# Recurrent attention and a two-level mixture of experts on one core: another order for the routing of two chunks, the first expert weights and the first unit

## The chip, the cores and the metric

One core of one Trainium2 chip runs the whole program. The metric is the device time of one execution in microseconds, as the median of several runs; lower is better. All other times are from one profiled execution of the kernel, counted from the start of its span.

## The reference, cut to what matters

A gated linear recurrence (four sequences, eight heads, 768 steps, head size 48) is followed by a mixture of 16 experts in four groups, in which each of the 3072 tokens goes to one expert.

```python
f = 1.0 / (1.0 + np.exp(-f_logit))
for t in range(S):
    state = f[:, :, t, :, None] * state + np.einsum('bhd,bhe->bhde', k[:, :, t], v[:, :, t])
    y[:, :, t] = np.einsum('bhd,bhde->bhe', q[:, :, t], state)
x = y.transpose(0, 2, 1, 3).reshape(B * S, H * D)          # 3072 x 384
g_idx = argmax(x @ w_group); g_w = softmax at g_idx
e_idx = argmax(x @ w_expert[g_idx]); e_w = softmax at e_idx
out[token] = g_w * e_w * (relu(x @ w1[g, e]) @ w2[g, e])   # 384 -> 1024 -> 384
```

## The kernel before, in words

**Attention.** The 768 steps are cut into six chunks of 128, and a chunk into two units of two sequences each; so there are twelve units, numbered 0 to 11. The work of a unit is written as small Python generators, each of which records a few instructions and yields: `bounded` (`c`, clamps the gate logits, L555), `gated` (`g`: exponential and logarithm on ScalarE, L565 and L568, then the running sum over time as a matmul, `cs`, L574, and two exponentials of it, `eq` and `kh`), `multiplied` (`m`: q times `eq`, L589, and k times `kh`, L592, on VectorE), `turned` (`t`: transposes `tr_q` and `tr_k` on TensorE, L604, copied to SBUF, L605), `decayed` (`b`: transposes `gt` of the row `ends`, L614), `scored` (`s`: the products `ap`, L630, masked into `am` by VectorE, L633), `weighed` (`w`: `y`, first from the state, L669, then from `am` and v, L674, copied to `xT`, L677), `stated` (`n`: the new state, `ds`, L647), `done` (`d`: routing logits `lT`, L689, `lgT`, L691, `lg`, L694) and `listed` (`x`: `x_ps`, L709, copied and written to `x_dram`, L712).

**Order.** The engines TensorE, VectorE and ScalarE run their instructions in the order in which these generators are advanced. That order is written out by hand: the strings `BEGIN`, `EVEN`, `ODD` and `ORDERS` name a generator and an offset to the unit, and `step` advances it once. `r` advances the oldest routing that is under way, `e` the early experts.

**Routing.** When both units of a chunk have their logits, `routed` starts `route` for it. It yields ten times at most: (1) maxima; (2) the one-hot `ohe`, L200; (3) ranks `rk` on TensorE, L205 and L208; (4) slots, `pick` to `run`, L214 to L217; (5) the lane mask `ln`, L227; (6) `head` and `val`, L231 and L234; (7) the weights and `meta`, L237 to L247, written to `x_dram`; (8) the table `tb` on TensorE, L252; (9) a ranking of the experts, L272 to L281, in some chunks only; (10) the sum into the table, L257, and what follows it. Chunk 3 (`CLOSE`) is the one after which the two fullest experts are fixed: `choose_early` writes their names into `who` (L290) and their first 128 rows into `rows_e`. With these, SyncE loads the weights of the two experts (`load_weights`, 1536 KB each of first layer `w1` and second layer `w2`, L384 and L386), GpSimd gathers the rows (L394), and `early` computes both experts: `up` (L440, `hp`) for the first and the second, and then `down_rows` (L457, `yo`) for each. Chunk 4's step 4 also runs `fix_early` (L300 to L306), and the last chunk's step 10 `choose`, whose gathers (`rows_p`) begin the sixteen main passes. The passes then take the rest of the time.

**Transfers.** SyncE issues all loads, ScalarE the writes of `x_dram<-x` and of `ends<-eq`, the last row of a unit's decay, which `gt` later transposes. Each of these transfers signals one of eight completion semaphores, which the compiler gives out; before a transfer is issued on a semaphore, its queue waits until the one before it on that semaphore has landed.

Of the kernel before, what the change touches and what calls it, by code (L numbers as in the profile page):

```python
# [10 lines left out]
FP32 = mybir.dt.float32  # L11
# [4 lines left out]
OP = mybir.AluOpType  # L16
AX = mybir.AxisListType.X
ET = mybir.EngineType
P = 128
# [4 lines left out]
def kernel(  # L24
# [12 lines left out]
    nc = tc.nc  # L37
    B, H, S, D = q.shape
    N, DM = out.shape
    G = moe_w_group.shape[1]  # L40
    EG = moe_w_expert.shape[2]
    F = moe_w1.shape[3]
    GE = G * EG
    NC = S // P
    NT = N // P
    HP = H // 2
    DP = 64
    KO = DM // P
    FO = F // P
    NL = G + GE  # L50
    WIDE = 2 * P
    EARLY = 2
# [9 lines left out]
    SAFE = 32.0  # L62
# [6 lines left out]
    wp = ctx.enter_context(tc.tile_pool(name="wp", bufs=2))  # L69
# [4 lines left out]
    w1v = moe_w1.rearrange("g e (ko p) f -> (g e) p ko f", p=P)  # L74
    w2v = moe_w2.rearrange("g e (fo p) d -> (g e) p fo d", p=P)

    def const(shape, dtype, name):
        return cp.tile(shape, dtype, tag=name, name=name)

    def bank(shape, name):  # L80
        return ps.tile(shape, FP32, tag="bank", name=name)
# [9 lines left out]
    ident = const([P, P], FP32, "ident")  # L91
# [170 lines left out]
    who = const([1, GE], I32, "who")  # L262
# [3 lines left out]
    def ranked(np_, sb):  # L266

        def tmp(shape, name):
            return sb.tile(shape, FP32, tag=name, bufs=1, name=name)

        key = tmp([P, GE], "rkey")
        nc.vector.tensor_tensor(key, run, base, OP.subtract)  # L272
        nc.vector.scalar_tensor_tensor(out=key, in0=key, scalar=float(GE), in1=tie, op0=OP.mult, op1=OP.add)
        if np_ > EARLY:
            nc.vector.tensor_tensor(key, key, boost, OP.add)
        less = tmp([P, GE, GE], "less")
        nc.vector.tensor_tensor(less, key.unsqueeze(1).broadcast_to((P, GE, GE)), key.unsqueeze(2).broadcast_to((P, GE, GE)), OP.is_gt)
        rank = tmp([P, GE], "rank")
        nc.vector.reduce_sum(out=rank, in_=less, axis=AX)
        sel = order[:, 0:np_, :]  # L280
        nc.vector.tensor_tensor(sel, rank.unsqueeze(1).broadcast_to((P, np_, GE)), experts[:, 0:np_].unsqueeze(2).broadcast_to((P, np_, GE)), OP.is_equal)  # L281
        return rank
# [30 lines left out]
    def choose_early(sb):  # L313
        number = numbers(sb)
        mine = sb.tile([P, EARLY, GE], FP32, tag="mine2", bufs=1, name="mine2")
        nc.vector.tensor_tensor(mine, order[:, 0:EARLY, :], number[:, :, 0].unsqueeze(1).broadcast_to((P, EARLY, GE)), OP.mult)
        got = sb.tile([P, EARLY], FP32, tag="got2", bufs=1, name="got2")
        nc.vector.reduce_sum(out=got, in_=mine, axis=AX)
        nc.vector.tensor_copy(rows_e, got)
        named(EARLY, sb)  # L320

    def choose(sb):
        number = numbers(sb)
        mine = sb.tile([P, 2, HP, P], FP32, tag="am", bufs=3, name="mine").rearrange("p r a t -> p (r a t)")[:, 0:2 * GE * GE].rearrange("p (n j e) -> p n j e", j=2, e=GE)
        got = sb.tile([P, GE, 2], FP32, tag="got", bufs=1, name="got")
        for j in range(2):
            nc.vector.tensor_tensor(mine[:, :, j, :], order, number[:, :, j].unsqueeze(1).broadcast_to((P, GE, GE)), OP.mult)
        nc.vector.reduce_sum(out=got, in_=mine, axis=AX)
        nc.vector.tensor_copy(rows_p, got)
        named(GE, sb)  # L330
# [47 lines left out]
    def value(ap, top):  # L378
        return nc.values_load(ap, engines=(ET.SP,), min_val=0, max_val=top, skip_runtime_bounds_check_because="a table that the routing makes within these bounds")

    def load_weights(pool, ap):
        e = value(ap, GE - 1)
        w1 = pool.tile([P, KO, F], FP32, tag="w1", name="w1")
        nc.sync.dma_start(out=w1, in_=w1v[bass.ds(e, 1)].rearrange("o p k f -> (o p) k f"))  # L384
        w2 = pool.tile([P, FO, DM], FP32, tag="w2", name="w2")
        nc.sync.dma_start(out=w2, in_=w2v[bass.ds(e, 1)].rearrange("o p k f -> (o p) k f"))  # L386
        return w1, w2

    def fetch(pool, rows, n, top=N):

# [96 lines left out]
    def early():  # L487

        ws = [fetch(ep, rows_e[:, p:p + 1], P, (CLOSE + 1) * B * P) for p in range(EARLY)]
        yield  # L490
        for w in ws:
            turn_in(w)
            yield
        for p, w in enumerate(ws):
            yield from up(w, weights[p][0])
        for p, w in enumerate(ws):
            yield from down_rows(w, weights[p][1])

    weights = {}

    with ExitStack() as fast:
# [27 lines left out]
        NU = len(units)  # L529
# [3 lines left out]
        def heads(t):  # L533
            return t.rearrange("p b h d -> p (b h) d")
# [23 lines left out]
        def gated(i):  # L558
# [13 lines left out]
            for b in range(2):  # L572
# [8 lines left out]
                    nc.scalar.dma_start(out=ends[c][2 * s:2 * s + 2, :], in_=eq[P - 1:P].rearrange("o b h d -> o b (h d)"))  # L581
                yield

        def multiplied(i):

            w = live[i]
            for b in (slice(0, 1), slice(1, 2)) if i < 2 else (slice(0, 2),):
                qh, kh = heads(w["qh"][:, b])[:, :, 0:D], heads(w["kh"][:, b])[:, :, 0:D]
                nc.vector.tensor_tensor(qh, qh, heads(w["eq"][:, b])[:, :, 0:D], OP.mult)  # L589
                yield  # L590

                nc.vector.scalar_tensor_tensor(out=kh, in0=kh, scalar=math.exp(SAFE), in1=heads(w["k"][:, b]), op0=OP.min, op1=OP.mult)  # L592
                yield

        def turned(i):
            w = live[i]
            w["g"] = decays[:, units[i][0], :, 2 * units[i][1]:2 * units[i][1] + 2].rearrange("p a b -> p b a")
            for nm in ("q", "k"):
                w["T" + nm] = sb.tile([P, 2, HP, P], FP32, tag="T" + nm, name="T" + nm)
            for b in range(2):  # L600
                for nm in ("q", "k"):
                    pt = bank([P, HP, P], "tr_" + nm)
                    for a in range(HP):
                        nc.tensor.transpose(out=pt[:, a, :], in_=w[nm + "h"][:, b, 2 * a:2 * a + 2, :].rearrange("t r d -> t (r d)"), identity=ident)  # L604
                    (nc.vector.tensor_copy if i == 0 and b == 0 and nm == "k" else nc.scalar.copy)(w["T" + nm][:, b], pt)  # L605
                    yield

        def decayed(i):

# [105 lines left out]
        def routed(c):  # L715

            yield from route(c, groups[c], sb, tidy=fix_early if c == CLOSE + 1 else None, ranking=rank_early if c == CLOSE else (lambda pool: ranked(GE, pool)) if c == NC - 1 else None)
            if c == CLOSE:
                choose_early(sb)
                for p in range(EARLY):  # L720
                    weights[p] = load_weights(wp, who[0:1, p:p + 1])
                first.append(early())
                next(first[0])
            elif c == NC - 1:
                choose(sb)

        def advance(gens):
            if gens and next(gens[0], True):
                gens.pop(0)

        first, routes = [], []

# [3 lines left out]
        STAGES = {"c": bounded, "g": gated, "m": multiplied, "t": turned, "s": scored, "n": stated, "w": weighed, "d": done, "x": listed, "b": decayed}  # L736
        BEGIN = """c0 g0 p g0 g0 m0 m0 m0 m0 l2 t0 t0 t0 t0 c1 g1 g1 s0 s0 s0 s0 g1 g1 p w0 w0 n0 m1 m1 m1 m1 l3 h x0 x0 x0
            t1 t1 t1 t1 b1 c2 g2 g2 s1 s1 s1 s1 p d0 g2 g2 n0 n1 w1 w1 m2 m2 l4 n1
            d0 x1 x1 t2 t2 t2 t2 c3 g3 g3 x1 s2 s2 s2 s2 g3 g3 w2 d1 w2 n2 m3 m3 c4 g4 g4""".split()
        BEGUN = 3  # L740
        EVEN = "l+2 d-2 n-1 r r r x-1 x-1 t t t t g+1 g+1 x-1 r s s s s c+2 w d-1 g+2 w g+2 n m+1 m+1".split()
        ODD = "l+2 d-2 b n-1 r r x-1 x-1 t t t t g+1 g+1 x-1 r s s s s c+2 w d-1 g+2 w g+2 n m+1 m+1 r n".split()
        ORDERS = {
            NU - 2: "d-2 r r r x-1 x-1 t t t t g+1 g+1 x-1 r s s s s w d-1 w n m+1 m+1 r r".split(),
            NU - 1: "d-2 b n-1 x-1 x-1 r r t t t t x-1 r s s s s r w d-1 w r r".split(),
            NU: "d-2 r e d-1 x-1 x-1 d-1 x-1 r r r e e r e r r e r r e r e r r e e e e e".split(),
        }
        steps_of = {}
# [1 line left out]
        def step(nm, i):  # L750
            if nm == "r":
                advance(routes)
            elif nm == "e":
                next(first[0], None)
            elif nm == "p":
                next(pad)
            elif nm == "h":
                turn_gates()
            elif 0 <= i < NU:
                if nm == "l":  # L760
                    load(i)
                    return
                if (nm, i) not in steps_of:
                    steps_of[nm, i] = STAGES[nm](i)
                next(steps_of[nm, i], None)
# [7 lines left out]
        for tok in BEGIN:  # L773
            step(tok[0], int(tok[1:] or 0))
# [43 lines left out]
    rest = const([1, 1], I32, "rest")  # L818
    ws = {n: pass_of(n) for n in range(3)}
    ahead = {n: load_weights(wq if n % 3 == 1 else wp, who[0:1, PLACES[n]:PLACES[n] + 1]) for n in range(1, 2)}  # L820
    ahead[0] = weights[0]

# [20 lines left out]
    for n in range(GE - 1):  # L843
        w = ws[n]
# [108 lines left out]
    with tc.If(more > 0), ExitStack() as late:  # L953
# [5 lines left out]
        with tc.For_i(0, last, 1) as i:  # L959
            w1, w2 = load_weights(wp, b_expert[0:1, bass.ds(i, 1)])  # L960
# [13 lines left out]
            w = fetch(ep, row, P)  # L974
# [32 lines left out]
```

## Time and profile before

| | |
|---|---|
| time, median of 3 runs | 436.17 us (435.5 to 436.47) |
| span of the profiled execution | 434.2 us |
| TensorE matmuls busy | 409.4 us, 94% |
| VectorE busy | 268.5 us, 62% |
| ScalarE busy | 154.5 us, 36% |
| GpSimd busy | 71.7 us, 17% |
| moved by DMA | 88.97 MB |

How to read the views: the page gives busy time by engine, then the span in 40 slices with busy tenths of each. The table of waits has on each line the waiting instruction, what ended its wait, the sum in us, how often, and the longest. The timeline has start, length, engine, line, operation, tiles and count, and in brackets the idle time ahead of it with what ended it. Neighbours of one kind are merged into one line.

In time order: attention fills 0 to some 142 us, the two early experts 145 to 169 us, and the sixteen passes the rest, with the last write landing at the end.

### The profile page before, as it was taken

The numbers are of one execution on the slowest core, as the hardware profiler recorded it, in microseconds if no ns is written. First come the engines' busy times: TensorE is split into PE (matmuls) and PEld (weight loads), VectorE is DVE, ScalarE is ACT, GpSimd is POOL, SyncE is SP. The second block draws the span as 40 slices with busy tenths as digits, with TensorE's granted clock in tenths as the row PEclk, the third lists the DMA queues.
The fourth block names the chain that finished last, engine by engine and source line by source line (L and its number), as shares of the span: only waits on it lengthen the run. The fifth ranks groups of instructions, "written<-read, shape, count | busy, mean of one in ns | idle before, by whom it ended". The sixth has DMA issues, their size and how long they took to land. (4 is left out here: it accounts for less than half of the span.)

```text
span 434.2 us, 10159 instructions
## 1 busy us (share of the span) xinstructions
PE 409.4 (94%) x4103; PEld 383.8 (88%) x4103; DVE 268.5 (62%) x781; ACT 154.5 (36%) x338; POOL 71.7 (17%) x109
## 2 busy tenths in 40 slices
PE   4999999999998989999999999999999999999960
PEld 2888999889998877989999999999999999999940
DVE  5675786778687841540799759468559558651500
ACT  5676765576664411211123123123123122222200
POOL 3000000000002037101031232212212211022120
PEclk9999999999999999999999999999999999999995
DMA  9999999999815979965728549468459558652010
GB/s 168 175 208 203 186 196 161 219 217 209 159 39 166 404 242 364 394 217 215 255 74 337 170 189 327 151 238 311 158 233 348 174 191 331 239 163 92 25 32 17
DMA packets 135232, 88.97 MB, mean 205 GB/s; under 512 B 105422, under 2 KB 125972, under 8 KB 135178
## 3 DMA queue, kind: packets, MB, share of 16 engines
q1 hardware_dynamic: 126754, 72.38, 61.2%
q0 software_dynamic: 5056, 11.06, 7.6%
q10 hardware_dynamic: 3368, 4.80, 3.1%
q8 instruction: 34, 0.56, 0.6%
q14 instruction: 20, 0.16, 0.1%
HBM read 78.71 MB, written 9.83 MB: 204 GB/s over the span
## 5 line engine op out<-in xcount | busy, mean ns | idle before, releaser
L440 PE MATMUL hp<-xe,w 128*128 128x128 f32 (+14 forms) x864 | 138.6, 320 | 1.6 <-DMA w<-in_moe_w_dram 1.6
L440 PEld LDWEIGHTS hp<-xe,w 128*128 128x128 f32 x864 | 135.8, 190 | 2.5 <-issue 1.7
L472 PE MATMUL yo<-h,w 128*128 128x230 f32 (+13 forms) x672 | 115.8, 333 | 0.0
L472 PEld LDWEIGHTS yo<-h,w 128*128 128x128 f32 x672 | 113.7, 190 | 0.2
L423 DVE STREAM_TRANSPOSE yr<-yT 32x192 f32<-32x192 f32 (+1 forms) x208 | 70.5, 339 | 64.7 <-ACT yT L473 62.1
L441 ACT ACTIVATE h<-hp 128x256 f32<-128x256 f32 (+14 forms) x72 | 34.4, 478 | 110.7 <-PE hp L440 110.7
L416 DVE STREAM_TRANSPOSE xe<-xg 32x192 f32<-32x192 f32 (+1 forms) x208 | 69.7, 335 | 5.0 <-PE hp L440 2.0
L451 POOL DMA_INDIRECT out_dram<-yt,xg x32 | 34.5, 1080 | 154.7 <-ACT yt L448 82.2
L473 ACT COPY yT<-yo 128x230 f32<-128x230 f32 (+13 forms) x42 | 13.5, 326 | 80.5 <-PE yo L472 80.5
L394 POOL DMA_INDIRECT xg<-x_dram,rows_p x30 | 29.6, 988 | 70.4 <-DMA out_dram<-yt,xg 22.8
L633 DVE TENSOR_TENSOR am<-ap,tri 128x512 f32<-128x512 f32 x48 | 29.8, 683 | 18.0 <-PE ap L630 18.0
L574 PE MATMUL cs<-ld_f,tri 128*128 128x384 f32 x48 | 19.2, 526 | 6.2 <-DVE ld_f L555 5.4
L630 PE MATMUL ap<-Tq,Tk 48*64 48x128 f32 x768 | 23.9, 273 | 0.1
L674 PE MATMUL y<-am,v 128*64 128x128 f32 x384 | 23.1, 273 | 0.0
L674 PEld LDWEIGHTS y<-am,v 128*64 128x64 f32 x384 | 21.3, 137 | 0.5 <-DVE am L633 0.5
L630 PEld LDWEIGHTS ap<-Tq,Tk 48*64 48x64 f32 x768 | 20.8, 133 | 1.0 <-issue 0.2
L457 PE MATMUL yo<-w,h 128*128 128x384 f32 x64 | 21.3, 486 | 0.0
L246 POOL COPY meta<-token 128x4 int32<-128x4 int32 x6 | 1.3, 218 | 109.0 <-DMA x_dram<-meta 109.0
L457 PEld LDWEIGHTS yo<-w,h 128*128 128x128 f32 x64 | 11.9, 190 | 7.4
L574 PEld LDWEIGHTS cs<-ld_f,tri 128*128 128x128 f32 x48 | 8.6, 200 | 10.4 <-POOL meta L246 5.4
L448 ACT ACTIVATE yt<-yr,xg 128x384 f32<-128x384 f32 (+13 forms) x26 | 14.4, 604 | 5.4 <-DVE yr L423 5.4
L677 ACT COPY xT<-y 128x512 f32<-128x512 f32 x24 | 12.9, 588 | 8.2 <-PE y L674 8.2
(168 smaller groups left out, 380.4 us busy)
## 6 DMA issues: line engine op xcount, KB each, us to landing
w<-in_moe_w_dram SPq DMA_DIRECT2D x34, 1536.0 KB, 11.0
qh<-in_q_dram SPq DMA_DIRECT2D x12, 384.0 KB, 8.0
ld_k<-in_k_dram SPq DMA_DIRECT2D x12, 384.0 KB, 7.8
v<-in_v_dram SPq DMA_DIRECT2D x12, 384.0 KB, 7.1
x_dram<-x ACTq DMA_DIRECT2D x12, 384.0 KB
ld_f<-in_f_logit_dram SPq DMA_DIRECT2D x11, 384.0 KB, 6.1
out_dram<-yt,xg POOLq DMA_INDIRECT x32, 3.8
xg<-x_dram,rows_p POOLq DMA_INDIRECT x30, 6.6
```

The lines of the kernel that those rows point to most:

```text
L394: nc.gpsimd.indirect_dma_start(out=w["x"][:, j, :], out_offset=None, in_=x_dram[0:1 + top, :], in_offset=bass.IndirectOffsetOnAxis(ap=rows ...
L416: squares(w, lambda n, k_, rk, g, rg: nc.vector.transpose(out=xT[rg, 0:n, k_], in_=x[rk, 0:n, g]))
L423: squares(w, lambda n, k_, rk, g, rg: nc.vector.transpose(out=y[rk, 0:n, g], in_=yT[rg, 0:n, k_]))
L440: nc.tensor.matmul(hp[:, o, :], lhsT=w1[:, ko, (f + o) * P:(f + o + 1) * P], rhs=w["xT"][:, ko, :], start=(ko == 0), stop=(ko == KO - 1))
L441: nc.scalar.activation(h[:, f:f + 2, :], hp, AF.Relu)
L451: nc.gpsimd.indirect_dma_start(out=out, out_offset=bass.IndirectOffsetOnAxis(ap=w["x"][0:m, j, DM + 1:RW].bitcast(U32), axis=0), in_=y[0:m ...
L457: nc.tensor.matmul(yp, lhsT=w["h"][:, fo, :], rhs=w2[:, fo, :], start=(fo == 0), stop=(fo == FO - 1))
L472: nc.tensor.matmul(yp, lhsT=w2[:, fo, m * P:(m + 1) * P], rhs=w["h"][:, fo, :], start=(fo == 0), stop=(fo == FO - 1))
L574: nc.tensor.matmul(cs.rearrange("t h d -> t (h d)"), lhsT=tri, rhs=nl[:, b], start=True, stop=True)
L630: nc.tensor.matmul(ap[r][half, a, :], lhsT=w["Tk"][rows, b, a, half], rhs=w["Tq"][rows, b, a, :], start=True, stop=True)
L633: nc.vector.tensor_tensor(am[:, r], ap[r], tri.unsqueeze(1).broadcast_to((P, HP, P)), OP.mult)
L674: nc.tensor.matmul(ys[r][DP * b:DP * b + DP, a, :], lhsT=w["v"][:, b, 2 * a + r, :], rhs=w["am"][b][:, r, a, :], start=(c == 0 and a == 0) ...
```

## The change

Four things are changed.

1. **Routing of chunks 3 and 4.** In unit 9's order two `r` move ahead of the score products, so that chunk 3's steps 3 to 6 come one place earlier; in unit 10's order the three `r` at its start are then steps 7, 8 and 9 (the ranking, L272 to L281, comes ahead of the mask `am`). In unit 11's order `q q` advances the second routing in the list, chunk 4's steps 1 and 2, and only then `r` takes chunk 3's step 10, which names the early experts. Then chunk 4's steps 3 and 4 come ahead of unit 11's score products, where step 4 stood behind them. The purpose is to have chunk 4's `ohe` ready when TensorE comes to `rk`.
2. **Early experts' weights.** Both numbers are read first, then the two first layers are loaded, and then the two second layers.
3. **First unit.** q of both sequences is multiplied, transposed and copied ahead of k, so that it need not wait for k; all four copies go to ScalarE, where one was VectorE's.
4. **Unit 2.** The first half of `weighed` (from the state) moves ahead of the running sums of unit 3.

```diff
+    def load_layer(pool, e, layer):
+        w = pool.tile([P, KO, F] if layer == 1 else [P, FO, DM], FP32, tag=f"w{layer}", name=f"w{layer}")
+        nc.sync.dma_start(out=w, in_=(w1v if layer == 1 else w2v)[bass.ds(e, 1)].rearrange("o p k f -> (o p) k f"))
+        return w
...
+        def in_order(i, bs):
+            return [(nm, b) for nm in ("q", "k") for b in bs] if i == 0 else [(nm, b) for b in bs for nm in ("q", "k")]
...
-            for b in range(2):
-                for nm in ("q", "k"):
...
-                    (nc.vector.tensor_copy if i == 0 and b == 0 and nm == "k" else nc.scalar.copy)(w["T" + nm][:, b], pt)
+            for nm, b in in_order(i, range(2)):
...
+                nc.scalar.copy(w["T" + nm][:, b], pt)
...
-                for p in range(EARLY):
-                    weights[p] = load_weights(wp, who[0:1, p:p + 1])
+                es = [value(who[0:1, p:p + 1], GE - 1) for p in range(EARLY)]
+                w1s, w2s = ([load_layer(wp, e, layer) for e in es] for layer in (1, 2))
+                weights.update(enumerate(zip(w1s, w2s)))
...
-        def advance(gens):
-            if gens and next(gens[0], True):
-                gens.pop(0)
+        def advance(gens, n=0):
+            if len(gens) > n and next(gens[n], True):
+                gens.pop(n)
...
-            d0 x1 x1 t2 t2 t2 t2 c3 g3 g3 x1 s2 s2 s2 s2 g3 g3 w2 d1 w2 n2 m3 m3 c4 g4 g4""".split()
+            d0 x1 x1 t2 t2 t2 t2 c3 g3 g3 x1 s2 s2 s2 s2 w2 g3 g3 d1 w2 n2 m3 m3 c4 g4 g4""".split()
...
-            NU - 2: "d-2 r r r x-1 x-1 t t t t g+1 g+1 x-1 r s s s s w d-1 w n m+1 m+1 r r".split(),
-            NU - 1: "d-2 b n-1 x-1 x-1 r r t t t t x-1 r s s s s r w d-1 w r r".split(),
+            NU - 3: "l+2 d-2 b n-1 r r x-1 x-1 t t t t r g+1 g+1 x-1 r r s s s s c+2 w d-1 g+2 w g+2 n m+1 m+1 r n".split(),
+            NU - 2: "d-2 r r r x-1 x-1 t t t t g+1 g+1 x-1 s s s s w d-1 w n m+1 m+1".split(),
+            NU - 1: "d-2 b q q r n-1 x-1 x-1 t t t t r x-1 r s s s s w d-1 w r r".split(),
```

## The prediction

> **What bounds the kernel now.** I read the page first, then the table of waits for TensorE, then the timeline around the waits, engine by engine.
>
> ```profile
> PE 409.4 (94%) x4103; PEld 383.8 (88%) x4103; DVE 268.5 (62%) x781; ACT 154.5 (36%) x338; POOL 71.7 (17%) x109
> ...
> DMA  9999999999815979965728549468459558652010
> ```
>
> TensorE works almost without a break, so a change counts only where it moves TensorE. The DMA row is the second message: up to slice 10 (some 110 us) the transfer engines are full too. TensorE's waits, from its table and from the timeline:
>
> ```profile
> PE cs L574 <- DVE ld_f L555: 5.4, 1, 5.4
> PE hp L440 <- DMA w<-in_moe_w_dram: 1.6, 1, 1.6
> PE rk L205 <- DVE ohe L200: 1.1, 1, 1.1
> PE cs L574 <- ACT ld_f L568: 0.8, 2, 0.5
> PE tr_k L604 <- DVE kh L592: 0.7, 1, 0.7
> PE x_ps L709 <- ACT xT L677: 0.4, 1, 0.4
> ```
>
> The change aims at five of these six lines: 1.1 (`rk`), 1.6 (`hp`), 0.5 of 0.8 (`cs` at 35.73) and the 0.7 of the first unit. They sum to some 4 us. What follows shows why most of it does not reach the end. Three more pieces of timeline are needed:
>
> ```profile
> 37.96 0.60 ACTq L581 DMA_DIRECT2D ends<-eq  x1
> 39.39 0.27 ACT L691 COPY lgT<-lT 128x128 f32<-128x128 f32 x1 [1.07 <-PE lT L689]
> ...
> 84.50 0.60 ACTq L581 DMA_DIRECT2D ends<-eq  x1
> 85.13 0.42 ACTq L712 DMA_DIRECT2D x_dram<-x  x1
> 85.59 0.27 ACT L691 COPY lgT<-lT 128x128 f32<-128x128 f32 x1 [3.93 <-DMA ends<-eq]
> ```
>
> The second `ends` shows a wait that no table of TensorE has: ScalarE stood 3.93 us, because this transfer waited for the load of q on its completion semaphore, which landed at 84.42, 0.08 us ahead of the issue.
>
> ```profile
> 41.13 0.56 DVE L555 TENSOR_SCALAR ld_f<-ld_f 128x768 f32<-128x768 f32 x1 [1.34 <-DMA ld_f<-in_f_logit_dram]
> ...
> 133.77 0.17 DVE L290 CAST who<-names 1x2 int32<-1x2 f32 x1
> ...
> 151.38 0.28 PE L252 MATMUL tb<-val,ln 128*128 128x64 bf16 x4
> 153.25 5.60 PE L440 MATMUL hp<-xe,w 128*128 128x128 f32 x48 [1.59 <-DMA w<-in_moe_w_dram]
> 158.68 8.55 PE L457 MATMUL yo<-w,h 128*128 128x384 f32 x26
> 167.07 0.49 PE L430 MATMUL xg_ps<-ident,xg 128*128 128x128 f32 x3
> ```
>
> Here the reader sees unit 4's gate logits landing at 41.1, the early experts named at 133.94, and TensorE full from 153.25 on; from 170 to 415 us it has no gap, so what is won by `xg_ps` at 167.07 is won at the end.
>
> [...]
>
> **First unit.** DVE's `kh` waits for k until 9.44 in both orders, but q of sequence 1 now goes in the gap. Then both k products are back to back and the last ends at 10.55 rather than 10.93. Four ScalarE copies of 0.59 run from 9.59: the first k copy ends at about 11.3, where VectorE's ended at 11.53. So `ap` starts about 0.3 to 0.4 us earlier.
>
> **Unit 2.** `y` from the state (0.99 us) fills the 0.51 us in which `cs` waits for the logarithm. 0.5 us more, so TensorE would reach `gt` (42.28 before) at about 41.5.
>
> **The new wait.** In the compiled order of the changed kernel the completion semaphores fall differently. Unit 3's `ends` shared one with q of unit 3, landed at 36.54; it now shares one with unit 4's gate logits, which land at 41.11. These loads don't follow TensorE: SyncE issues them back to back, 1.5 to 3.9 us each, with queues full. So ScalarE stands until 41.18, and behind it stand `lgT` (for `lg`) and the copies `xT`; and `gt` needs the landed row itself. From issue to landing the `ends` rows took 3.4, 3.1, 3.3, 1.7, 2.0, 1.9, 2.7, 2.4 and 2.6 us while the queues were full: mean 2.6, ends 1.7 and 3.4. So `gt` starts at 41.18 + 2.6 = 43.8, between 42.9 and 44.6: 1.5 us (0.6 to 2.3) later than before, and the two gains above are gone.
> Some of that is given back. Before, TensorE was held by the load stream twice: `x_ps` at 76.25 (about 0.3 us late) and at 88.05 (0.5; the page of waits has 0.4). A later TensorE arrives after these loads. 1.5 - 0.8 = 0.7 us remains at 90 us (0 to 1.5). I call it d.
>
> **Routing.** Unit 9: `rk` comes right behind the transposes, at 113.13 + d, when `ohe` is ready (113.05 + d): at most 0.1. Steps 4 and 5 take 0.8 + 1.5 = 2.3 us between 113.6 and 115.9, where VectorE was idle until `am` at 115.92: they just fit. Unit 10: steps 5 and 6 have left, the ranking (1.5 us) came, before `am` at 126.79: fits; `tb` (0.2) only changes place. Unit 11: `lg` at 131.20 gives the logits at 131.65; steps 1 and 2 take 1.94 us (133.85 to 135.79 before), so `ohe` is ready at 133.6, and `rk` runs when the transposes end, at 134.56, instead of 135.84: 1.28 won. But step 10 now stands behind: 133.6 + 1.58 (132.36 to 133.94 before) gives `who` at 135.2, **1.24 us later**. Step 4 with `fix_early` (1.68 us) follows, so `am` starts at 136.8, not at the 136.04 that `ap` would allow; before it was 137.35. TensorE's `y` waits for `am`, so 0.57 of the 1.28 is left: everything to the early experts is 0.57 earlier.
>
> **Weights.** The first w1 was issued at 134.66 and landed at 144.48; the others landed at 148.2, 153.1 and 156.9. Now the first issue is at 135.9. The 384 KB write of ScalarE now goes ahead of the weights rather than among them, which gives back 0.4 us or so; so all landings are 0.8 later (0.4 to 1.24). First w1: 145.3; `hp` would be ready at 144.8 (145.36 - 0.57); it starts at about 145.3, no gain left. Its up-projection and the routing matmuls take 6.3 us as before, to 151.6. The second w1 is now the second to land, at about 149: the 1.59 us wait is gone, in full (1.65 with the start-up). w2 is needed at 157 and lands by 154. So `yo` begins 1.7 us earlier.
> Then comes `xg_ps`. Its rows are gathered by GpSimd, which waited for the last `meta` writes; they landed at 157.27 and 157.65, behind the weights in the queues, the gather was issued at 158.51 and landed at 165.16, 1.9 us ahead of need. With the queues drained 0.8 us later it lands at 166.0, while TensorE now wants it at 165.4: a new wait of 0.6. **The gain at 167.07 is 1.1 us** (0.7 to 1.5).
>
> Sum: 0.7 - 1.1 = -0.4 us, so 435.8.
>
> **The rivals.** (a) *Both waits go, nothing comes in*: the 1.12 and 1.59 are in the profile and their removal by order is plain. If the `ends` row lands in 1.7 us, d is 0, and with the weights only 0.4 late the gain is 1.5: 434.7. With `who` not late either, 2.7 us: 433.5. Against it: `who` is behind six VectorE operations that it wasn't behind before. (b) *No measurable change*, the sum above: 435.8. (c) *Slower*: `gt` held for 3.4 us of landing, d = 1.5; weights a full 1.24 late, gain 0.7: +0.8, 437.0; if the early delay isn't absorbed, +1.5: 437.7. For it: ScalarE's order and the semaphores are fixed by the program, and the 3.93 us at 84.50 shows that such a wait is paid. (d) *The start gains count after all* (the loads land earlier too): -0.8 more, 435.0. Against it: the DMA row is 9 from the first slice.
>
> **How the numbers follow.** Within 0.2% is 435.30 to 437.04. (b) has 0.48. (a) and (d) have 0.38 together: the landing of `ends` is the widest term, and below 2 us it lies on their side. (c) has 0.14. The range is from 434.6, (a) with half a chance of a still better `who` left out, to 437.0, the first case of (c).
>
> **What would show it.** Right: in the changed kernel's waits, `rk <- ohe` and `hp <- DMA w` gone or short; `gt` (or `lg`) waiting near 42 us with `ends` issued at about 41.2; `who` at about 135 plus d; a wait at `xg_ps` near 166 us for the gather. Wrong: `ends` of unit 3 issued at about 38 us; `xg_ps` early and unwaited; a wait after 170 us, where I expect none.

## The result, and the profile after

The changed kernel takes 441.03 us (median of 4 runs, 439.28 to 442.11), the kernel before 436.32 us on the same chip: 1.0107 of it, 95% interval 1.0069 to 1.0144. It is 4.7 us slower. All medians and intervals here are of fast executions; one slow one of e7 (867.66 us) and one of e14 (542.65 us) are left out. The span of the profiled run went from 434.2 to 438.8 us. (In the changed file most lines stand one to five further down: `cs` L575, `ends` L582, `gt` L619.)

TensorE's waits in the changed kernel, by releaser (total, times, longest; those of the first units and two of 0.3 us are left out):

```profile
PE gt L619 <- DMA ends<-eq: 2.9, 1, 2.9
PE lg L699 <- ACT lgT L696: 2.5, 1, 2.5
PE xg_ps L431 <- POOL yT L835: 1.2, 1, 1.2
PE hp L441 <- DMA w<-in_moe_w_dram: 0.4, 1, 0.4
```

The four waits that the change aims at are gone or nearly so (`rk` 1.1, `cs` 0.5 and `tr_k` 0.7 are gone, the second expert's 1.6 at `hp` is gone too, and the 0.4 there now is the first expert's). Two new ones of 5.4 us together stand ahead of `lg` and `gt`, between 40.7 and 46.6 us; the one at `xg_ps` was expected. ScalarE's timeline at the start of the two (start, length, then in brackets the idle time before and its releaser):

```profile
37.55 0.51 ACT L577 ACTIVATE kh<-cs 128x384 f32<-128x384 f32 x1
42.28 0.61 ACTq L582 DMA_DIRECT2D ends<-eq  x1
42.93 0.27 ACT L696 COPY lgT<-lT 128x128 f32<-128x128 f32 x1 [4.86 <-DMA ld_f<-in_f_logit_dram]
```

`ends` of unit 3 goes out at 42.28 us, 4.3 us later than before, once unit 4's gate logits (`ld_f`) have landed; `lgT`, which needs no transfer at all, is behind it. TensorE pays for both:

```profile
39.63 1.09 PE L652 MATMUL ds<-v,kh 128*64 128x48 f32 x32
43.25 0.41 PE L699 MATMUL lg<-fold,lgT 128*128 128x40 f32 x2 [2.53 <-ACT lgT L696]
46.55 0.56 PE L619 MATMUL gt<-ident,ends 4*128 4x4 f32 x4 [2.89 <-DMA ends<-eq]
47.04 1.97 PE L714 MATMUL x_ps<-ident,xT 128*128 128x128 f32 x8
```

The last line is a second effect: the same eight transposes took 1.09 us in the kernel before:

```profile
42.28 0.41 PE L614 MATMUL gt<-ident,ends 4*128 4x4 f32 x4
42.62 1.09 PE L709 MATMUL x_ps<-ident,xT 128*128 128x128 f32 x8
```

The table by stretches of 2 us says why, in its column PEclk:

```profile
core 0: us, PE busy (x) PEld busy (x) DVE busy (x) ACT busy (x) POOL busy (x), PEclk, DMA share, GB/s
40.00:42.00 2.00, 0.72 (x26) 0.59 (x22) 0.00 (x0) 0.00 (x0) 0.00 (x0) 1.00 0.68 136
42.00:44.00 2.00, 0.41 (x2) 0.30 (x2) 0.86 (x3) 1.07 (x3) 0.00 (x0) 0.94 1.27 243
44.00:46.00 2.00, 0.00 (x0) 0.00 (x0) 0.36 (x1) 1.75 (x3) 0.00 (x0) 0.50 1.50 166
48.00:50.00 2.00, 2.00 (x11) 2.00 (x10) 1.24 (x6) 1.06 (x3) 0.00 (x0) 0.50 1.35 218
50.00:52.00 2.00, 2.00 (x14) 1.82 (x13) 0.00 (x0) 1.73 (x4) 0.00 (x0) 0.85 1.42 220
```

TensorE stood for most of 40.7 to 46.5 us, and its granted clock fell to half from 43.8 to 50.6 us. In the kernel before it was 1.00 there in every stretch, for example:

```profile
44.00:46.00 2.00, 2.00 (x17) 1.74 (x16) 1.59 (x7) 2.00 (x6) 0.00 (x0) 1.00 1.50 163
```

How late TensorE is, against the kernel before, at four places (start of the same group of matmuls in both timelines, us):

```
                         before    changed
cs of unit 4              45.30     +6.13     4.27 of standing, 1.86 of half clock
cs of unit 8              90.78     +5.35     0.78 absorbed by the load stream
gt of the last chunk     131.55     +5.69
xg_ps of the main part   167.07     +4.81     routing and weights won 0.88
```

From there to 204 us the difference stays at 4.84. So by this profile routing and weights (points 1 and 2 of the change) won 0.9 us, and 6.1 us were lost ahead of them, at the start. The lines of routing and weights in the timeline of all engines:

```profile
140.51 0.16 DVE L290 CAST who<-names 1x2 int32<-1x2 f32 x1
...
150.78 1.61 PE L441 MATMUL hp<-xe,w 128*128 128x128 f32 x12 [0.43 <-DMA w<-in_moe_w_dram]
...
171.88 0.52 PE L431 MATMUL xg_ps<-ident,xg 128*128 128x128 f32 x3 [1.16 <-POOL yT L835]
```

The names come 6.74 us later than before while TensorE at 131.55 is 5.69 late, so 1.05 later in its terms, and the main part's gather holds `xg_ps` for 1.16 us. (The line names GpSimd's `yT`, which was done at 171.53. The gather's rows landed at 171.58, 0.30 us ahead of `xg_ps`, and in e2 and e5 they landed 0.30 us ahead of it too.)

### The profile page after: what moved, and what is told of

Same layout as the page of the kernel before. It is cut to its first block, busy times and chain, and to the rows that moved or that the text cites. A ratio compares the mean times of both kernels' runs of the same rounds, so it can differ in the third digit from the quotient of the medians.

```text
span 438.8 us, 10156 instructions
## 1 busy us (share of the span) xinstructions
PE 411.3 (94%) x4103; PEld 385.7 (88%) x4103; DVE 268.1 (61%) x780; ACT 156.3 (36%) x339; POOL 71.6 (16%) x109
## 5 line engine op out<-in xcount | busy, mean ns | idle before, releaser
L575 PE MATMUL cs<-ld_f,tri 128*128 128x384 f32 x48 | 19.3, 527 | 5.4 <-ACT ld_f L569 5.2
L575 PEld LDWEIGHTS cs<-ld_f,tri 128*128 128x128 f32 x48 | 8.6, 200 | 9.5 <-POOL meta L246 5.2
```

What stands on the lines that cost most here:

```text
L575: nc.tensor.matmul(cs.rearrange("t h d -> t (h d)"), lhsT=tri, rhs=nl[:, b], start=True, stop=True)
```

## The experiments

Theory: in the compiled program `ends` of unit 3 shares its completion semaphore with unit 4's gate logits; ScalarE waits for them, TensorE for ScalarE and for the row, and then runs at half clock. The traces bear the sharing out, since each transfer's record carries its semaphore. In the trace of the kernel before and in that of the changed kernel SyncE's and ScalarE's transfers carry eight different ones, and each of the 109 transfers (in either trace) that has an earlier one on its semaphore was issued after that one had landed: 0.02 us after at the closest, 0.08 for `ends` of unit 3 in the changed kernel. In the changed kernel, e3, e4, e5 and e7 the transfer before `ends` on its semaphore is unit 4's gate logits, in all other profiles q or v of unit 3. So it takes the first unit's and unit 2's new order together (or e3's extra loads); either alone (e6, e11) doesn't bring it. Rival 1: the routing's new order (late names, gather behind the weights) costs the time. Rival 2: the new order at the start costs by itself. The runs were made in four groups of four, each group on one chip beside runs of the kernel before.

Places that TensorE reaches, late (+) or early (-) in us against the trace of the kernel before, from one profile each. A profiled run needn't be typical of its group: the mean granted clock of an execution was 0.984 or less in every profile in which the clock fell ahead of the end, and 0.986 or more in every other (at the end the kernel before has half clock too, from 422.2 us on). The counts of falls among the executions that have no profile are estimates from these mean clocks. The first two units scatter from -0.4 to +1.4 us between profiles of one and the same start, so differences between columns count more than a number by itself. "Won" is the column before it less the last:

```
                      45.30    90.78   131.55   167.07     won      time ratio (95% interval)
changed               +6.13    +5.35    +5.69    +4.81     0.88     1.0107 (1.0069 to 1.0144)
e1 row later          -1.08    +1.31    +1.41    +0.33     1.08     1.0053 (1.0031 to 1.0075)
e2 routing, weights   -0.36    -1.14    -1.04    -1.18     0.14     1.0004 (0.9987 to 1.0020)
e3 split loads        +2.36    +1.57    +1.57    +1.64    -0.07     1.0081 (1.0054 to 1.0107)
e4 filled             +3.86    +3.08    +3.19    +1.99     1.20     1.0086 (1.0053 to 1.0119)
e5 changed again      +6.08    +5.30    +5.40    +4.51     0.89     1.0118 (1.0098 to 1.0138)
e6 no y swap          -0.28    +3.52    +3.68    +2.85     0.83     1.0063 (1.0040 to 1.0086)
e7 start only         +7.13    +6.61    +6.61    +6.55     0.06     1.0124 (1.0100 to 1.0148)
e8 names first        -0.22    -0.08    +0.02    -3.02     3.04     0.9940 (0.9921 to 0.9958)
e9 routing only       -0.27    -0.76    -0.65    -0.28    -0.37     1.0038 (1.0024 to 1.0052)
e10 weights only      +0.15    -0.64    -0.15    -1.80     1.65     1.0044 (1.0028 to 1.0059)
e11 no first unit     +1.86    +1.07    +1.18    +0.70     0.48     1.0042 (1.0023 to 1.0061)
e12 names first, y    -0.52    +0.01    +0.11    -2.87     2.98     0.9995 (0.9980 to 1.0009)
e13 routing only      -0.26    -1.04    -0.94    -0.19    -0.75     1.0026 (1.0015 to 1.0037)
e14 weights only      -0.18    -0.96    -0.96    -2.63     1.67     1.0033 (1.0020 to 1.0045)
e15 no first unit     -0.83    -0.86    -0.76    -1.57     0.81     1.0050 (1.0034 to 1.0066)
e16 names first       +1.44    +0.66    +0.76    -2.24     3.00     0.9978 (0.9966 to 0.9990)
```

**e1: two small writes a unit later.**

```diff
-            if i == BEGUN:
+            if i == BEGUN + 1:
                 nc.sync.dma_start(out=x_dram[0:1, 0:DM]...
```

> The changed kernel, but the two small writes of the zero row of x_dram are issued one unit later. Nothing else moves; only the count of transfers ahead of unit 3's ends falls by two, so that ends shares its completion semaphore with unit 3's v (landed some 38 us) and no longer with unit 4's gate logits (42.2 us). Theory (the shared semaphore costs the time): ends is issued by 39 us rather than 42.28, gt starts near 42 us rather than 46.55, and with the 0.9 us won in routing and weights the time is 435.4 us (434.9 to 436.2). Rival 1 (the routing's new order, the late names of the early experts, the gather behind the weights): all of that is still there, so 440 us or more. Rival 2 (the first unit's q ahead of its k and the y moved ahead of cs bring the loads out of step): also still there, 440 us or more.

Measured 437.25 us against 435.19, above the expected range and below what the rivals say. `ends` went out at 37.92 us and `gt` ran at 41.20: the stand is gone and TensorE was 1.08 us ahead. But 3 us went again by 60 us. SyncE's queue and VectorE show where to:

```profile
42.67 2.17 SPq L550 DMA_DIRECT2D qh<-in_q_dram  x1
45.01 2.22 SPq L550 DMA_DIRECT2D ld_f<-in_f_logit_dram  x1
```

```profile
53.33 0.56 DVE L556 TENSOR_SCALAR ld_f<-ld_f 128x768 f32<-128x768 f32 x1 [3.60 <-DMA ld_f<-in_f_logit_dram]
```

My edit moved unit 5's q ahead of its gate logits in the load queue, so these landed at 53.3 rather than 50.8 us. The run shows the wait's part; its total doesn't, since it added a fault of its own.

**e2: routing and weights alone.** The hunks of `load_layer`, `advance` and `ORDERS`, without those of `in_order`, `turned` and `BEGIN`.

> The kernel before with only the routing orders and the order of the early experts' weight loads changed; first unit and unit 2 as before. Unit 3's ends keeps its old partner (q of unit 3, 36.5 us). Theory: 435.4 us, the 0.9 us of gain alone, the rk wait and the 1.6 us hp wait gone, a wait of about 1 us at xg_ps for the gather. Rival 1 (routing): 440 us or more. Rival 2 (the start): 435.4 us, so that this run does not tell it from the theory.

435.33 against 435.19 us. Rival 1 falls: with all of the routing's and weights' change, nothing is lost. But the gain was 0.14 us, not 0.9: `xg_ps` stood twice, 0.88 us for the early gather and 1.27 for the main one (the second line names a load; the gather's rows landed at 165.59). With TensorE on time, more of what is won at `rk` and `hp` is waited away.

```profile
141.05 0.52 PE L431 MATMUL xg_ps<-ident,xg 128*128 128x128 f32 x3 [0.88 <-DMA xg<-x_dram,rows_e]
165.89 0.52 PE L431 MATMUL xg_ps<-ident,xg 128*128 128x128 f32 x3 [1.27 <-DMA w<-in_moe_w_dram]
```

**e3: only the suspected sharing, in the kernel before.**

```diff
-                for b in parts(i) if nm == "f" else (slice(0, 2),):
+                for b in (slice(0, 1), slice(1, 2)) if i == 4 and nm != "f" else parts(i) if nm == "f" else (slice(0, 2),):
```

> The kernel before, with unit 4's loads of q, k and v issued as two halves each: three transfers more, the same bytes. No part of the change is in it, but unit 3's ends now shares its completion semaphore with unit 4's gate logits. Theory: ends issued at 41 to 42 us, gt at 45 to 46.5 us, TensorE's clock falls after the stand, and the time is 439.8 to 441.8 us (436.3 + 6.1 - 0.8 at most). Rivals 1 and 2: 436.3 us, since neither the routing nor the start is changed.

438.05 against 435.19 us, where the rivals expect no difference. `ends` was held as in the changed kernel:

```profile
41.76 0.60 ACTq L581 DMA_DIRECT2D ends<-eq  x1
```

```profile
44.67 0.38 PE L614 MATMUL gt<-ident,ends 4*128 4x4 f32 x4 [0.98 <-DMA ends<-eq]
```

The stand was only 0.98 us here: in this profile TensorE had come 1.3 us late from the first unit, and `gt` started 2.9 us after the row's issue rather than 4.3. The clock stayed at 1.00. Of ten executions the two longest (440.2 and 440.6 us) had mean clocks of 0.978 and 0.982, the other eight 0.985 to 0.989. The loss is below the expected range and not in full the theory's, as the split also touches three loads; and of the 1.64 us at 167.07 in this profile 1.3 are the lateness of the first unit. So e3 shows that the sharing holds `ends` and `gt` without any part of the change; what it costs in full, it doesn't show.

**e4: the stands filled.**

```diff
+            if i == 1:      # lb: the bank of lg, its columns 128 to 255
+                for _ in range(8):
+                    nc.tensor.matmul(lb[:, P:2 * P], lhsT=tri, rhs=ident, start=True, stop=True)
 ...
+                if i == 3:  # gb: the bank of gt
+                    for _ in range(10):
+                        nc.tensor.matmul(gb[:, P:2 * P], lhsT=tri, rhs=ident, start=True, stop=True)
```

> The changed kernel with matmuls of no use (18 of 128x128, some 4.7 us) on TensorE in the two stands ahead of lg and gt near 41 to 46 us, into columns of the same banks that nothing reads. If the fall of TensorE's granted clock to 0.5 after the stand costs its own 1.9 us, the clock stays at 1.0, x_ps takes 1.1 us rather than 1.97, and the time is 439.1 us (438.6 to 439.8). If the clock is only how the stand shows in the records, or falls for another reason: 441.0 us.

438.01 us against 435.19, ratio 1.0086, where the changed kernel has 1.0118 on another chip (e5). This doesn't decide: the two intervals overlap, and the expected 439.1 and 441.0 us are 1.0064 and 1.0107 of the 436.32 us that the kernel before took in the first comparison, with the measured ratio between them. In one of the six executions (440.73 us, mean clock 0.982) the clock fell all the same. The profile tells more. The stretches:

```profile
44.00:46.00 2.00, 1.61 (x15) 1.42 (x13) 0.00 (x1) 1.40 (x2) 0.00 (x0) 1.00 1.51 167
46.00:48.00 2.00, 1.82 (x18) 1.84 (x19) 1.14 (x4) 0.99 (x3) 0.00 (x0) 1.00 1.44 175
48.00:50.00 2.00, 2.00 (x16) 1.74 (x14) 0.75 (x4) 2.00 (x5) 0.00 (x0) 1.00 1.34 218
```

```profile
46.18 0.38 PE L623 MATMUL gt<-ident,ends 4*128 4x4 f32 x4 [0.56 <-DMA ends<-eq]
46.49 1.09 PE L722 MATMUL x_ps<-ident,xT 128*128 128x128 f32 x8
```

PEclk is 1.00 throughout, `x_ps` took 1.09 us, and `gt` still waited for the row, issued at 41.92, until 46.18. From there to `cs` of unit 4 TensorE's lateness stays (3.90, then 3.86), while it grows from 4.27 to 6.13 in the changed kernel and from 4.11 to 6.08 in e5. So the half clock is a cost of its own, 1.9 us; that the useless work made the whole kernel faster is likely, but not shown by the times.

**e5: the changed kernel again.**

> The changed kernel once more, beside the others on one chip, as their yardstick. Theory: slower than the kernel before by 3.5 to 6 us; ends of unit 3 issued at 42 us after unit 4's gate logits, gt near 46 us. In executions in which the stand is long TensorE's granted clock falls and the mean clock of the execution is 0.985 or less; the times spread by some 3 us for that reason.

440.91 against 435.88 us; `ends` at 42.10, `gt` at 46.39, mean clocks 0.978 to 0.984.

**e6: unit 2's order undone.**

```diff
-            ... c3 g3 g3 x1 s2 s2 s2 s2 w2 g3 g3 d1 w2 ...
+            ... c3 g3 g3 x1 s2 s2 s2 s2 g3 g3 w2 d1 w2 ...
```

> The changed kernel without the change in unit 2 (y ahead of cs): routing, weights and the first unit as changed. By the compiled order unit 3's ends then shares its completion semaphore with unit 3's v (landed near 38 us) rather than unit 4's gate logits; the loads keep their order, which the run with the later row did not. Theory: gt starts by 42 us, no stand, and the time is that of the run with routing and weights alone, within 0.5 us of the kernel before (the 0.3 us of the first unit end in the load stream). Rivals (routing, or the first unit's new order, cost time by themselves): slower than before by 2 us or more.

438.93 against 435.88 us, so it misses, and lies where the rivals said. No stand at `gt` (42.01 us), and TensorE is 0.28 us early up to 69 us. Then it stands at 76, and the clock falls again (`x_ps` 1.97):

```profile
78.72 1.97 PE L714 MATMUL x_ps<-ident,xT 128*128 128x128 f32 x8 [2.81 <-ACT xT L682]
```

ScalarE had waited for unit 7's gate logits. SyncE's queue, in this kernel and below it in e2:

```profile
66.49 1.43 SPq L550 DMA_DIRECT2D qh<-in_q_dram  x1
68.02 1.99 SPq L247 DMA_DIRECT2D x_dram<-meta  x1
70.10 0.47 SPq L550 DMA_DIRECT2D ld_f<-in_f_logit_dram  x1
```

```profile
65.02 1.82 SPq L247 DMA_DIRECT2D x_dram<-meta  x1
66.94 0.49 SPq L550 DMA_DIRECT2D ld_f<-in_f_logit_dram  x1
67.48 1.42 SPq L550 DMA_DIRECT2D qh<-in_q_dram  x1
```

The compiled order has unit 7's q ahead of its gate logits. The compiled programs place it so in the changed kernel and in e1, e6 and e7, and not in the kernel before, e2, e8, e11 and e12: it comes with the first unit's new order. In the changed kernel it costs nothing, because TensorE is 6 us late by then. A second fault lay hidden behind the first. It doesn't strike in every execution: eight of the twelve have a mean clock of 0.985 or less (median 439.22 us), and the other four took 435.87 to 436.77 us, close to what was expected.

**e7: first unit and unit 2 alone.** The hunks of `in_order`, `multiplied`, `turned` and `BEGIN`.

> The kernel before with the first unit's q ahead of its k and unit 2's y ahead of cs; routing and weights as before. Unit 3's ends shares its completion semaphore with unit 4's gate logits. Theory: all of the loss is here: as the changed kernel or up to 1 us slower than it (the routing's and weights' gain is missing), so 4 to 6.5 us slower than before. Rival (the routing's new order costs the time): no slower than before.

440.94 against 435.88 us (median of five executions), as expected. All of the loss is in these two parts, so rival 2 is right about the place; the theory says how. `gt` came 4.49 us late, and the half clock lasted 10.2 us:

```profile
46.77 0.55 PE L618 MATMUL gt<-ident,ends 4*128 4x4 f32 x4 [2.63 <-DMA ends<-eq]
```

**e8: names first.** e2 with one line more:

```diff
-            NU - 1: "d-2 b q q r n-1 x-1 x-1 t t t t r x-1 r s s s s w d-1 w r r".split(),
+            NU - 1: "r d-2 b r r n-1 x-1 x-1 t t t t r x-1 r s s s s w d-1 w r r".split(),
```

> Routing and weights as changed, first unit and unit 2 as before, and in the order of unit 11 the last step of the fourth chunk's routing (which names the early experts) put ahead of the last logits instead of behind the fifth chunk's first two steps. Theory of the routing's end: there the chain from the names over the weights and the meta writes to the gather ends last; so the names come 2 us earlier relative to TensorE, the waits at xg_ps (0.9 and 1.3 us) and at hp (0.45 us) shrink, and the time is 1.5 to 2.6 us below that of the run with routing and weights alone: 432.8 to 434 us on the same chip. Rival: that stretch is bound by TensorE's own work or by the drain of the weights, whatever the names do: no change, 435.3 us.

433.09 against 435.88 us, 0.9940 of it, as expected: faster than both kernels. All that is left in TensorE's table of waits is of the start and the load stream; `rk`, `hp` and `xg_ps` are not in it:

```profile
PE cs L575 <- ACT ld_f L569: 6.1, 3, 5.3
PE tr_k L605 <- DVE kh L593: 0.6, 1, 0.6
PE x_ps L710 <- ACT xT L678: 0.4, 1, 0.4
```

**e9 to e12: single parts, and e8 with unit 2's y.** e9 is the routing orders alone, e10 `load_layer` and the new order of loads alone, e11 the changed kernel without the first unit's hunks, e12 is e11 with e8's line.

> The kernel before with only the routing orders changed; the weights are loaded as before (first and second layer of one expert, then of the other), first unit and unit 2 as before. Theory: rk comes 1.3 us earlier, but the names of the early experts come 1.2 us later relative to TensorE, so weights and gather end where they ended, the wait for the second expert's first layer grows from 1.6 to about 2.9 us, and the time is that of before within 0.5 us. Rival: the 1.3 us count by themselves, 1.3 us faster.

> The kernel before with only the order of the early experts' weight loads changed (both first layers, then both second layers). The names come as early as before. Theory: the 1.6 us wait at hp goes, the gather, landed 1.9 us ahead of its need before, is now just in time: 1.0 to 1.6 us faster than before, and so faster than with the routing's new order on top. Rival: the drain of the weights holds TensorE wherever they stand, no gain.

> The changed kernel without the first unit's new order: routing, weights and unit 2's y ahead of cs as changed. Unit 3's ends shares its completion semaphore with unit 3's v (landed near 38 us), and in the compiled order no q stands ahead of its unit's gate logits (as unit 7's did in the run without unit 2's y, and unit 5's in the run with the later row). Theory: no stand at gt, none at x_ps near 76 us, TensorE's clock stays at 1.0 after the first unit, and the time is that of routing and weights alone, within 0.6 us of before. Rival (y ahead of cs costs by itself): 2 us or more slower.

> As the run without the first unit's new order, with the last step of the fourth chunk's routing ahead of the last logits (names first). Theory: both causes are out of the way; 2.4 to 3.2 us faster than before, as in the run with names first, since what unit 2's y wins ends in the load stream by 90 us. Rival: unit 2's 0.5 us count after all: 0.5 us faster than that run.

The kernel before took 436.94 us here; e9 438.43, e10 438.59, e11 439.10, e12 437.06: every one misses its expected time, and e11 lies 2.2 us above the kernel before, where its rival is. Up to 170 us the profiles agree with the expectations in the main, with two exceptions. In e9 TensorE lost two times 0.4 us inside `ap` near 136 us with no releaser on record (e11 and e13 too), and by `xg_ps` e9 has lost 0.37 us. In e11 and e12 `gt` still stood for the row, issued at 39.69 and 39.05 us after unit 3's v:

```profile
44.17 0.38 PE L615 MATMUL gt<-ident,ends 4*128 4x4 f32 x4 [1.13 <-DMA ends<-eq]
```

```profile
41.80 0.38 PE L615 MATMUL gt<-ident,ends 4*128 4x4 f32 x4 [0.59 <-DMA ends<-eq]
```

The clock did not fall there: `x_ps` behind it took 1.09 us in both. Then all four stop at 170 to 176 us, where no earlier profile shows a stop. TensorE and VectorE of e12:

```profile
172.84 0.27 PE L441 MATMUL hp<-xe,w 128*128 128x128 f32 x1 [0.91 <-issue]
```

```profile
174.37 0.94 DVE L432 COPY xe<-xg_ps 128x384 f32<-128x384 f32 x2 [9.03 <-remote]
```

e9, e10 and e12 reach `yo` (184.63 before) at 186.1 to 186.5 us whether they came 0.3 or 2.9 us early. What is won by 167 us does not count in these profiles.

**e13 to e16: the same parts, and e8, on a fourth chip.** The kernels of e9, e10, e11 and e8.

> The kernel with only the routing orders changed, once more, for its time without the stop at 170 to 175 us that the last four profiles had. Theory (names late eat the earlier rk): within 0.6 us of before, xg_ps near 167 us unmoved. Rival (the 1.3 us of rk count): 1 us or more faster.

> The kernel with only the weights' order changed, once more, for the same reason. Theory: no wait at hp for the second expert, 1.0 to 1.8 us faster than before; so the routing's new order loses at the end what the weights' order wins, since both together were 0.0% off. Rival: no gain.

> The changed kernel without the first unit's new order, once more, for the same reason. Theory: within 0.8 us of before (ends issued by 39.7 us, gt at most 1.2 us late, nothing at x_ps near 76 us, clock 1.0): so the first unit's order, through the places that it moves in the compiled order, is what makes the change slow. Rival: 2 us or more slower, y ahead of cs costs by itself.

> The version that beat the kernel before, on this chip: routing and weights as changed, names first, start as before. Theory: 2 to 3 us faster than before, no wait at hp and xg_ps. If the stop at 170 to 175 us is the chip's and not a kernel's, it shows here too whenever it shows in the other three.

438.50, 438.76, 439.42 and 436.64 against 437.45 us: all four are slower than expected. The stop is in all four again, e8's kernel too, which ran without it in its first group. So it isn't of one kernel; its releaser is not in the records, which are incomplete there, and the kernel before has no profile from these chips. That leaves open how much of the times of e9 to e16 is the stop, and so whether weights alone would be faster than before without it.

The mean clocks tell one thing more. On these two chips none of the 103 executions of the kernel before has one of 0.985 or less, of the routing alone (e9, e13) 3 of 35, but of the six runs with the weights' new order 60 of 93. In the three profiles of these in which the clock fell (e11, e12, e16, with mean clocks of 0.983, 0.984 and 0.983), it fell right behind the stop: in e12 PEclk was 0.96 from 172 to 176 us and 0.62 from 176 to 180, which is 3.4 us of half clock; behind the stop three `hp` took 1.52 us in e11 and 19 took 5.38 us in e16, where 25 took 4.52 us in e13. So the weights' new order meets the stop in a way that costs half clock more often; why is open.

Up to 167 us the four chips agree: routing alone loses 0.4 to 0.8 us there, the weights' order alone wins 1.7, both together win 0.1 to 1.2, and with the names first 3.0 in every one of three profiles. e15's profile speaks for the theory at the start: without the first unit's order nothing stands at `gt` or at 76 us, and TensorE is 0.76 us early at 131.55, where the changed kernel is 5.69 late. It is one of six executions (median 437.82 us) without a fall of the clock; the other sixteen (439.96) have one, whose place no profile of e15 shows. Behind the stop is the likely place, since e14, without y ahead of `cs`, has a fall in 17 of 21. But that y ahead of `cs` costs something by itself is not excluded by the times: e15 is 2.0 us slower than before. e16 is still faster than before, by 0.2%.

## Why the prediction was wrong

The forecast was 435.8 us (434.6 to 437.0); the result of 441.03 lies 4 us above the range. (It says that the change aims at five of the six waits; it names and sums four.)

- **First unit**, 0.3 to 0.4 us: 0.41 in the changed kernel's profile (`ap` at 11.27 rather than 11.68). But kernels without it came 0.2 to 0.4 early as often, so it isn't told apart from the spread.
- **Unit 2**, 0.5 us: e1 went from 0.34 us early in the first units to 1.08 at `gt`, e15 from 0.09 to 0.83: 0.7, a little more than said. But it doesn't last: at `cs` of unit 6 (67.64 us before) e15 is 0.08 early.
- **The new wait**: this step failed. The place, the partner and the two engines were right; "1.5 us (0.6 to 2.3) later" became 4.27, and 6.13 with the clock. Three terms were off. First, the gate logits landed at 42.2 rather than 41.11: I took the landing of the kernel before as fixed (1.1 us). Second, the row took 4.3 us from issue to `gt` in four of five such profiles (changed, e4, e5, e7) and 2.9 in the fifth (e3), where 2.6 was said (1.7 us). The upper end of 3.4 was too low already by the trace of the kernel before: the list leaves out unit 0's row, issued at 8.84 us, which took 4.7. Why the row takes so long just here stays open. Third, 1.86 us of half clock was in no step at all.
- **Absorbed by the load stream**, 0.8 us: 0.78. Right, and TensorE's lateness hid unit 7's q, which I hadn't seen.
- **Routing**: `rk` won 1.28 (5.69 to 4.41 late between 131.55 and `rk`), as said; names 1.05 later in TensorE's terms, 1.24 said; of the 1.28 only 0.27 was left at `hp`, 0.57 said.
- **Weights**: the second expert's wait gone, `hp` of the first nearly without gain, as said; `yo` began 2.2 us earlier in TensorE's terms, 1.7 said. No run shows by itself the 0.4 us that the write of ScalarE was to give back. In the changed kernel that write was issued at 140.51 us, 0.9 ahead of the first weights, and landed at 143.32; the four weights landed 9.34, 13.08, 17.86 and 21.79 us after the first issue, 0.46 to 0.59 less than in the kernel before.
- **The new wait at `xg_ps`**, 0.6: 1.16, and 0.4 to 1.4 in seven other profiles with both parts. So the gain at 167.07 was 0.88, where 1.1 (0.7 to 1.5) was said; on time, in e2, only 0.14. With 6.13 for the new wait the prediction's own sum, 6.13 - 0.78 - 0.88, is 4.5, near the 4.7 that was measured.

Of the rivals (c), given a chance of 0.14, had the right side, and its own largest case, 437.7, was still 3.3 us short: it took the same landing and no clock.

ScalarE's wait behind `ends`, taken over from the 3.93 us of the kernel before, was there with 4.86 us. Half clock was not in the forecast at all: PEclk was 0.50 from 43.8 to 50.6 us in the changed kernel, 6.8 us, and for 6.8 us in e5, 10.2 in e7 and 3.4 in e6.

## What to carry to other kernels

When an edit changes where transfers are issued, compare the compiled programs for two things: which earlier transfer each one's completion semaphore belongs to, and the order of the loads; here a late partner held ScalarE for 4.86 us with all behind it, and the delay hid a second fault, which cost 2.81 us at `x_ps` in e6. Where TensorE stands, look at its granted clock too: the stand of 2.81 us in e6 brought 3.4 us of half clock, the one of 0.98 us in e3 none. And put the step that starts the longest chain of transfers (here the names, weights, rows) ahead of the step that feeds TensorE next, if TensorE can wait a little: the one moved step of e8 brought what the change was meant to bring, 0.6% on the chip without the stop and 0.2% on one with it (e12, with unit 2's y, 0.0%).

## What the runs showed of the hardware that was not expected

TensorE was not idle all the time ahead of a fall of its clock. In the 3.4 us ahead of it (as long as the shortest falls, those of e6 and e12) its busy share was 0.23 (changed), 0.30 (e5), 0.22 (e6), 0.43 (e7) and, near 172 us, 0.45 (e12). But idle time of that size doesn't always bring a fall: in e10 TensorE was busy for 0.58 of the 2.94 us from 173.75 to 176.69 us, and PEclk was 1.00 in every stretch from 164 to 188 us. What decides, these runs don't show.

On two of the chips TensorE and VectorE stopped together near 172 us, with no releaser on record (in e12 VectorE stood 9.03 us ahead of its copy of `xe`, 4.33 in e8, and ScalarE ran one instruction from 168 to 172 us where it ran three in e8), and TensorE lost 1.8 to 4.7 us between 167 us and `yo` (half clock included); in the profiles from the others never.
